# Constant matmuls in TensorE's early gaps, and an instruction order planned with them

## The chip, the core and the metric

The kernel runs on one core of a Trainium2 chip. The core has five engines that run side by side, each with its own instruction queue worked off in order: TensorE (PE in the profile; its weight loads are shown as PEld), VectorE (DVE), ScalarE (ACT), GpSimd (POOL) and SyncE (SP), which here only issues transfers between HBM and the on-chip memory SBUF. TensorE writes its results to another on-chip memory, PSUM, and VectorE or ScalarE copy them from there to SBUF.

The metric is the device time of one execution in microseconds (us). One execution is taken with a hardware profiler; its span goes from the first to the last instruction, and its own time is a little longer than its span.

## The reference

```python
x = A_q                                                    # (1, 2048, 640), bf16
k_shift = sum over t of k_pad[:, t:t+S, :] * shift_k[:, 3-t]     # a causal filter of 4 taps
kv = k_shift * v
y  = causal convolution of kv with ssm_k along the 2048 positions (by FFT of 4096, per channel)
h  = x + layernorm(x) * (y + kv * ssm_D)
h2 = h + (silu(layernorm(h) @ w_gate) * (layernorm(h) @ w_up)) @ w_down
```

There are 2048 positions of 640 channels. The feed-forward part has an inner width of 1728. Inputs and output are bf16.

## The kernel before

**Tiling.** The positions are cut into four blocks of 512 (block 0 to 3), each laid on 128 partitions as 4 slots of 640 channels. A block goes through a convolution stage (tags C0 to C3 in the code) and a feed-forward stage (F0 to F3).

**The convolution** is done in the frequency domain by matmuls with constant tables of cosines and sines. Each 512-position slice p of the filter ssm_k (tags G0 to G3) is loaded, folded by VectorE (`g_fold`, L701 to L713), turned by TensorE transposes into PSUM and copied out (`g_turn_pe`, L670 and L672), and transformed by matmuls with the table gb_t (`g_transform`, L736). For slice 0 the skip term ssm_D is added by one further matmul with the constant tile ones1, which has ones in its first row and zeros elsewhere. VectorE forms the 4 taps and the product with v (`shift`, L769 to L775). The product is transformed by matmuls with the table cs_t (`x_transform`: L792 for block 0, which also uses csm_t, the negated sines; L809 for the others). Copies out of PSUM go through one helper (`evac`, L437 on ScalarE, L443 on VectorE). VectorE multiplies spectra and adds them over earlier blocks; spectra that do not fit are written to HBM by GpSimd's queue and loaded again. `back` transforms back with the table ci_t (L901), scales and adds (L905, L909), takes the statistics of the layernorm (`ln_stats`: L838 and L840 on ScalarE, L849 to L852 on VectorE, the power -1/2 on GpSimd, L854), normalises (L921 or L924), and turns the result into the tile hlnT, by TensorE transposes for blocks 0 to 2 (L936), by transfers for block 3.

**The feed-forward stage** has 14 pieces of gate and up matmuls of 512 columns (L1009, ten for a full piece), ScalarE's silu and copy (L1013, L1014), VectorE's product (L1016), then the down matmuls (L1033, with h added through the identity in L1030 for blocks 0 to 2), ScalarE's copy out (L1038) and GpSimd's store.

**At the start** the four tap rows of shift_k, loaded into the first partition of a tile, are spread over the 128 partitions by eight matmuls with ones1 as weights (L529, 320 columns each) into four PSUM tiles, which are copied out as w, two by VectorE and two by ScalarE. ones1 is written by VectorE (L522, L523). ScalarE then takes the statistics of block 0's input (L838, L840 on wk), while VectorE forms the taps.

**Storage.** PSUM is used as four tiles of two banks (class `ps`). SBUF tiles belong to classes of a fixed count (five `wk`, three `wgu`, two `h`, and so on). Within every class except `ps`, tiles are handed out in the order in which the code creates them.

**The order of the work** is planned when the program is built. Every operation is put on record with its engine, a cost in us, what it reads and writes, and a priority; `DELTA` holds offsets to the priorities, one for a key of tag, engine and name, found beforehand. `Plan.schedule` is a list scheduler: for every engine it takes, among the operations whose inputs are done, the one that can start first, with lower priority number ahead on ties (with a slack of 0.05 us per unit of "slack SP", SP takes nearly always the lowest number). It keeps a clock per engine, starting at 0.6 us, and hands an operation a PSUM tile: of those free at its start, the one that came free last. TensorE's half-speed phase after a pause is modelled in four lines (`cold`). In the end the operations are sorted by planned start and issued in that order; each engine runs its own in that order on the chip, waiting by semaphores for what it needs.

Of the kernel before, what the change touches and what calls it, by code (L numbers as in the profile page):

```python
# [12 lines left out]
ACT = mybir.ActivationFunctionType  # L13
# [7 lines left out]
P = 128  # L21
# [6 lines left out]
GC = 256  # L28
NG = 7
DELTA = {  # L30
    "C0 ACT half": 5713,
    "C0 ACT lnh0": 1462,
    "C0 ACT y": 1339,
    "C0 ACT z": -2549,
    "C0 DVE eo0": -2261,
    "C0 DVE gate": -16818,
    "C0 DVE prod0": -14678,
    "C0 DVE tinyx": 31,
    "C0 PE inv0": -2297,
    "C0 SP ci_t": 16022,  # L40
    "C0 SP cs_t": 3931,
    "C0 SP gb_t": 1107,
    "C0 SP k": -728,
    "C0 SP v": -11,
    "C0 SP x": -2141,
    "C1 ACT hn": 2424,
    "C1 ACT xev1": -969,
    "C1 ACT y": -4984,
    "C1 DVE bfly0": -24238,
    "C1 DVE bfly1": -22972,  # L50
    "C1 DVE eo0": -3933,
    "C1 DVE eo1": -21519,
    "C1 DVE hmul0": -24066,
    "C1 DVE hmul1": -17335,
    "C1 DVE join0": -4523,
    "C1 DVE last": -3933,
    "C1 DVE nm": -14579,
    "C1 DVE prod": 733,
    "C1 DVE tinyh1": -3279,
    "C1 DVE xsum0": -3000,  # L60
    "C1 PE hTtr": -11983,
    "C2 ACT hn": -6262,
    "C2 DVE eo0": -12365,
    "C2 DVE eo1": -13863,
    "C2 DVE gate": -18349,
    "C2 DVE hmul0": -4317,
    "C2 DVE join0": -14364,
    "C2 DVE last": -99,
    "C2 DVE nm": 22411,
    "C2 DVE prod": -4774,  # L70
    "C2 DVE tinyx": -180,
    "C2 DVE xsum0": -668,
    "C2 DVE xsum1": -2435,
    "C3 ACT hn": -8326,
    "C3 ACT lnh0": 10,
    "C3 ACT lnh1": -9704,
    "C3 DVE bfly1": 20,
    "C3 DVE comb": 3729,
    "C3 DVE psum": -4522,
    "C3 DVE shift": 2173,  # L80
    "C3 DVE xsum1": 3949,
    "C3 PE x1": -26875,
    "C3 SP ldX": -5040,
    "F0 DVE ffn": -3823,
    "F0 PE down": 1944,
    "F0 SP w": 1894,
    "F1 PE down": 3501,
    "F2 DVE ffn": 2826,
    "G0 ACT gev": -234,
    "G0 DVE g_fold": -2452,  # L90
    "G0 DVE skip": -2446,
    "G0 PE g_transform": -10973,
    "G1 ACT gev": 13784,
    "G1 ACT half": 1293,
    "G1 DVE g_fold": -5018,
    "G2 ACT gev": 14649,
    "G2 DVE g_sum": 2060,
    "G2 PE g_turn_pe": 6402,
    "G3 DVE g_fold": -1695,
    "G3 DVE g_sum": 2144,  # L100
    "G3 PE g_transform": -6565,
    "slack SP": 3733,
}
OPT = (True, (0, 1, 2), (0,), (), (0, 1, 2), (1, 2, 3), True, (0,), (0,), 0, (0, 1, 2))

# [67 lines left out]


class Op:
    __slots__ = ("i", "eng", "dur", "fn", "deps", "succ", "allocs", "frees", "pri", "nwait", "ready", "soft", "alts", "key", "start", "end", "tag", "nbytes", "fix")


class Plan:
# [25 lines left out]
    def op(self, eng, dur, fn, r=(), w=(), pri=None, nbytes=0, alloc=(), alt=(), name=None, fix=None):  # L205
        o = Op()
        o.i, o.eng, o.dur, o.fn, o.nbytes = len(self.ops), eng, dur, fn, nbytes
        o.alts = [(eng, dur, fn)] + list(alt)
        o.fix = self.DMA_FIX if fix is None else fix
        o.pri = self.pri if pri is None else pri  # L210
        o.tag = self.tag
        o.key = f"{o.tag} {eng} {name or fn.__qualname__.split('.<locals>')[1 if fn.__qualname__.count('<locals>') > 1 else 0][1:]}"
        o.pri += DELTA.get(o.key, 0)
        o.deps, o.succ, o.soft, o.allocs, o.frees = set(), [], [], [], []
        for x, wr in [(x, False) for x in r] + [(x, True) for x in w] + [((b, 0), True) for b in alloc]:
            b, m = x if isinstance(x, tuple) else (x, -1)
            if b.cls is not None and o not in b.users:
                b.users.append(o)
            for i, bm, bw in b.log:
                if bm & m and (wr or bw):  # L220
                    o.deps.add(i)
            b.log.append((o.i, m, wr))
        o.deps.discard(o.i)
        self.ops.append(o)
        return o

    def schedule(self):
# [38 lines left out]
        while done < len(ops):  # L266
            best = None
            for e, lst in pend.items():
                cand = None
                t0 = clock[e]  # L270
                for o in lst:
                    st = max(t0, o.ready)
                    if o.nbytes:
                        st = max(st, flight[e != "POOL"][-8])
                        if e != "POOL":
                            st = max(st, hw_free)
                    ok = True
                    for b in o.allocs:
                        if not b.cls.startswith("ps") and fifo[b.cls][0] is not b and not (len(o.allocs) > 1 and b in fifo[b.cls][:len(o.allocs)]):
                            ok = False  # L280
                            break
                        if not free[b.cls]:
                            ok = False
                            break
                        st = max(st, min(free[b.cls])[0])
                    if not ok:
                        continue
                    key = (max(st, t0 + self.slack.get(e, 0)), o.pri, st, o.i)
                    if cand is None or key < cand[0]:
                        cand = (key, st, o, e)  # L290
                if cand and (best is None or cand[1] < best[1]):
                    best = cand
            if best is None:
                raise RuntimeError("plan stuck: " + repr([(e, [(o.i, o.tag, [b.name for b in o.allocs]) for o in l][:5]) for e, l in pend.items()])
                                   + repr({c: [b.name for b in f[:2]] for c, f in fifo.items()}))
            _, st, o, e = best
            o.eng, o.dur, o.fn = next(x for x in o.alts if x[0] == e)
            for b in o.allocs:
                if not b.cls.startswith("ps"):
                    fifo[b.cls].remove(b)  # L300
                k = min((x for x in free[b.cls] if x[0] <= st), key=lambda x: (-x[0], x[1]))
# [46 lines left out]
def kernel(  # L348
# [14 lines left out]
    nc = tc.nc  # L363
# [7 lines left out]
    psum = ctx.enter_context(tc.tile_pool(name="ps", bufs=1, space=bass.MemoryType.PSUM))  # L371
# [782 lines left out]
    order = pl.schedule()  # L1154
    with tc.manual_schedule():
        for o in order:
            o.fn()


# [28 lines left out]
```

## Time and profile before

| | |
|---|---|
| median of 8 runs | 297.24 us (295.34 to 297.82) |
| profiled execution: its own time | 296.66 us |
| profiled execution: span | 294.9 us |
| TensorE busy | 259.0 us, 1564 matmuls |
| VectorE busy | 217.5 us, 300 instructions |
| ScalarE busy | 213.4 us, 377 instructions |
| GpSimd busy | 31.2 us, 38 instructions |
| TensorE's first matmul | 3.10 us |
| TensorE's last matmul ends | 288.59 us |

A line of the summary gives an engine's busy time, its share of the span and its instructions. The row of digits under it cuts the span into 40 equal slices, and each digit is the busy share of a slice in tenths. A line of waits gives who waited for whom, the total in us, how many times, and the longest. The chain that ended last is followed back from the last instruction to whatever released it; its lines have a start, a length and what ran. In a timeline, "x16" merges 16 instructions, and a matmul's printed length includes its way through the array, so the pace of a row of matmuls is read from the distance of their starts. "L736" is a line of the kernel.

### The profile page before, as it was taken

The numbers are of one execution on the slowest core, as the hardware profiler recorded it, in microseconds if no ns is written. First come the engines' busy times: TensorE is split into PE (matmuls) and PEld (weight loads), VectorE is DVE, ScalarE is ACT, GpSimd is POOL, SyncE is SP. The second block draws the span as 40 slices with busy tenths as digits, with TensorE's granted clock in tenths as the row PEclk, the third lists the DMA queues.
The fourth block names the chain that finished last, engine by engine and source line by source line (L and its number), as shares of the span: only waits on it lengthen the run. The fifth ranks groups of instructions, "written<-read, shape, count | busy, mean of one in ns | idle before, by whom it ended". The sixth has DMA issues, their size and how long they took to land.

```text
span 294.9 us, 4255 instructions
## 1 busy us (share of the span) xinstructions
PE 259.0 (88%) x1564; PEld 150.2 (51%) x1564; DVE 217.5 (74%) x300; ACT 213.4 (72%) x377; POOL 31.2 (11%) x38
## 2 busy tenths in 40 slices
PE   3069998388999999899998998999999989999991
PEld 1046766154445576644444665654446754444670
DVE  5995999989999899899998998389998201121111
ACT  3588999989995978998558999961665973545321
POOL 2002001230102023011000030200000011000000
PEclk9999999869999999999999999999999999999998
DMA  7997158993994599934638798955563053550011
GB/s 228 344 372 243 50 226 258 373 380 129 293 329 103 185 353 390 381 103 133 153 71 240 233 314 314 327 195 134 114 177 89 2 133 106 145 129 0 2 44 46
DMA packets 59158, 57.83 MB, mean 196 GB/s; under 512 B 17729, under 2 KB 53762, under 8 KB 59138
## 3 DMA queue, kind: packets, MB, share of 16 engines
q1 hardware_dynamic: 57342, 47.08, 52.4%
q0 software_dynamic: 1792, 10.49, 9.5%
q8 instruction: 12, 0.20, 0.3%
q14 instruction: 8, 0.07, 0.1%
q10 hardware_dynamic: 4, 0.01, 0.0%
HBM read 45.76 MB, written 10.49 MB: 191 GB/s over the span
## 4 chain that ended last, share of the span: by engine, by line
ACT 36%; PE 30%; issue 19%; DVE 7%; DMA 5%; POOL 1%; SPq 1%; POOLq 0%; ACTq 0%; DVEq 0%
PE ps L1009 15%; ACT junk L838 6%; ACT lane L437 5%; PE ps L1033 5%; ACT junk L840 5%; PE ps L792 3%; DMA wk<-in_A_q_dram 3%; PE ps L736 3%; ACT s L905 3%; ACT sg L1013 2%; ACT s L921 2%; PE ps L809 2%; ACT uc L1014 2%; DMA lane<-xd 2%; ACT lane L745 2%
## 5 line engine op out<-in xcount | busy, mean ns | idle before, releaser
L1009 PE MATMUL ps<-hlnT,wgu 128*128 128x512 bf16 x540 | 119.0, 379 | 2.0 <-ACT uc L1014 1.1
L1009 PEld LDWEIGHTS <-wgu 128*128 128x128 bf16 x540 | 52.7, 98 | 66.1 <-issue 4.6
L1013 ACT ACTIVATE sg<-ps 128x512 bf16<-128x512 f32 (+1 forms) x56 | 33.6, 600 | 43.9 <-PE ps L1009 25.4
L1033 PE MATMUL ps<-wdA,tT 128*128 128x320 bf16 x384 | 55.6, 299 | 0.1
L1033 PEld LDWEIGHTS <-tT 128*128 128x128 bf16 x448 | 43.8, 98 | 17.4 <-issue 0.4
L1016 DVE TENSOR_TENSOR tT<-sg,uc 128x512 bf16<-128x512 bf16 (+1 forms) x56 | 22.8, 423 | 38.1 <-ACT uc L1014 37.9
L854 POOL TENSOR_TENSOR mv<-mv,mhalf 128x2 f32<-128x2 f32 (+1 forms) x12 | 18.6, 1552 | 146.7 <-DVE mv L850 81.4
L1014 ACT CAST uc<-ps 128x512 bf16<-128x512 f32 (+1 forms) x56 | 32.7, 584 | 0.3 <-PE ps L1009 0.2
L437 ACT CAST lane<-ps 128x640 bf16<-128x640 f32 x42 | 27.2, 745 | 0.9 <-PE ps L792 0.9
L1122 DVE TENSOR_TENSOR lane<-lane,lane 128x3840 bf16<-128x3840 bf16 x12 | 25.8, 2154 | 0.5 <-DMA lane<-hd 0.3
L736 PE MATMUL ps<-wgu,gb_t 128*128 128x320 bf16 x128 | 22.3, 312 | 3.8 <-ACT wgu L672 2.7
L769 DVE TENSOR_TENSOR wk<-krun,w 128x2560 bf16<-128x2560 bf16 (+1 forms) x20 | 24.0, 1220 | 0.0
L1038 ACT ACTIVATE o<-ps,mean 128x640 bf16<-128x640 f32 x16 | 12.5, 787 | 14.4 <-PE ps L1033 14.4
L809 PE MATMUL ps<-wk,cs_t 128*128 128x320 bf16 x96 | 17.1, 326 | 6.6 <-DVE wk L775 4.9
L901 PE MATMUL ps<-eo,ci_t 128*128 128x320 bf16 x128 | 18.7, 299 | 1.6 <-DMA wgu<-in_B_w_up_dram 1.0
L736 PEld LDWEIGHTS <-gb_t 128*128 128x128 bf16 x128 | 12.9, 101 | 11.2 <-issue 4.4
L774 DVE TENSOR_TENSOR wk<-wk,wk 128x2560 bf16<-128x2560 bf16 (+1 forms) x15 | 18.0, 1220 | 0.0
L901 PEld LDWEIGHTS <-ci_t 128*128 128x128 bf16 x128 | 12.5, 98 | 7.0 <-issue 1.9
L809 PEld LDWEIGHTS <-cs_t 128*128 128x128 bf16 x96 | 9.8, 104 | 12.1 <-DVE wk L775 5.2
L838 ACT ACTIVATE junk<-wk 128x640 bf16<-128x640 bf16 x16 | 11.9, 747 | 4.7 <-DMA wk<-in_A_q_dram 4.5
L905 ACT ACTIVATE s<-ps,one,mv 128x640 bf16<-128x640 f32 x15 | 13.3, 921 | 1.8 <-POOL mv L854 0.9
L838 ACT ACTIVATE junk<-h 128x640 bf16<-128x640 bf16 x16 | 12.0, 749 | 2.0 <-DVE h L909 1.5
(94 smaller groups left out, 311.4 us busy)
## 6 DMA issues: line engine op xcount, KB each, us to landing
wgu<-in_B_w_gate_dram SPq DMA_DIRECT2D x24, 320.0 KB, 3.3
wgu<-in_B_w_up_dram SPq DMA_DIRECT2D x24, 320.0 KB, 4.5
lane<-xd SPq DMA_DIRECT2D x6, 960.0 KB, 5.6
lane<-hd SPq DMA_DIRECT2D x6, 960.0 KB, 7.8
xd<-lane POOLq DMA_DIRECT2D x4, 960.0 KB, 5.1
hd<-lane POOLq DMA_DIRECT2D x4, 960.0 KB, 7.1
krun<-in_A_k_dram SPq DMA_DIRECT2D x4, 640.0 KB, 6.8
wk<-in_A_v_dram SPq DMA_DIRECT2D x4, 640.0 KB, 8.8
```

The costliest lines, as they stand in the source:

```text
L437: nc.scalar.copy(dst(), src())
L736: nc.tensor.matmul(ps.t[:, h, 0:NH], wt, mv, start=(k == 0), stop=(k == len(ks) - 1))
L769: nc.vector.tensor_mul(dst.t[:, sl, :], ks, w4.t[:, j:j + 1, :].broadcast_to([P, n, D]))
L809: nc.tensor.matmul(ps.t[:, h, 0:NH], cs_t.t[:, s, n, c * P:(c + 1) * P], kv.t[:, s, h * NH:(h + 1) * NH], start=(a == 0), stop=(a == 1))
L838: act(0.73, lambda s=s: nc.scalar.activation(junk.t[:], x.t[:, s, :], ACT.Identity, scale=-1.0 / D, accum_out=mv.t[:, s:s + 1]), [(x, 1 << ...
L901: nc.tensor.matmul(ps.t[:, hh, 0:NH], ci_t.t[:, c, 1 - n, s, :], x.t[:, 2 * pos[n] + c, hh * NH:(hh + 1) * NH], start=(k == 0), stop=(k == 3))
L1009: nc.tensor.matmul(q(ps.t[:, k, 0:w]), wg.t[:, kt, off:off + P], rr(hT.t[:, kt, :]), start=(kt == 0), stop=(kt == NDC - 1))
L1013: act(c_act(w) + 0.02, lambda ps=ps, sg=sg, np_=np_, w=w: nc.scalar.activation(sg.t[0:np_, 0:w], ps.t[0:np_, 0, 0:w], ACT.Silu), [(ps, 1)] ...
L1014: act(c_act(w), lambda ps=ps, uc=uc, np_=np_, lo=up_lo, k=len(offs) - 1, w=w: nc.scalar.copy(uc.t[0:np_, 0:w], ps.t[lo:lo + np_, k, 0:w]), ...
L1016: dve(c_tt(w), lambda sg=sg, uc=uc, c=c, np_=np_, w=w, rr=rr, q=q: nc.vector.tensor_mul(rr(tv()[0:np_, c, :]), q(sg.t[0:np_, 0:w]), q(uc.t ...
L1033: nc.tensor.matmul(ps.t[:, hh, 0:NH], tv()[:, c, m * P:(m + 1) * P], wdc(c)[:, hh * NH:(hh + 1) * NH], start=(c == 0 and not oadd), stop=( ...
L1122: dve(c_tt(6 * D), lambda xl=xl, hl=hl: nc.vector.tensor_mul(xl.t[:], xl.t[:], hl.t[:]), [xl(), hl()], [xl()], name="prod")
```

## The change

Three things are changed. Before an operation of TensorE that the plan starts more than 0.8 us after TensorE's last one, and that takes a new PSUM tile, a number of matmuls are issued into the first half of that same tile: weights ones1, and ones1 repeated four times as the 512 columns. What they write is overwritten by the operation itself. Their number is worked out in the plan from the planned start, the moment the tile came free, and 0.22 us for one. The model of the half-speed phase is changed: it now counts only a pause that can't be filled so, of over 2.5 us, and lasts 4.5 us instead of 2.6. And the table of offsets is another one.

```diff
-    "C0 SP ci_t": 16022,
-    "C0 SP cs_t": 3931,
-    "C0 SP gb_t": 1107,
...
+    "C0 DVE eo0": -46193,
+    "C0 SP cs_t": 6082,
+    "C0 SP k": -10520,
+    "C0 SP v": -3881,
+    "C0 SP x": -5367,
+    "C2 SP ldX": -18099,
+    "C3 DVE prod": -117764,
+    "G0 ACT turn": -130,
+    "G0 DVE g_fold": -302,
+    "slack SP": 13090,
...
-        o.deps, o.succ, o.soft, o.allocs, o.frees = set(), [], [], [], []
+        o.deps, o.succ, o.soft, o.allocs, o.frees, o.warm = set(), [], [], [], [], 0
...
                 b.slotno = k[1]
+                b.since = k[0]
             o.start = st
             if e == "PE":
-                if st - clock[e] > 2.0:
-                    cold = st + 2.6
+
+                since = max([b.since for b in o.allocs if b.cls == "ps"] or [st])
+                lo = max(min(since, st), clock[e])
+                if lo - clock[e] > 2.5:
+                    cold = st + 4.5
+                o.warm = max(0, int((st - 0.4 - lo) / 0.22)) if st - clock[e] > 0.8 else 0
                 if st < cold:
                     o.dur = 2 * o.dur if st + 2 * o.dur <= cold else o.dur + (cold - st) / 2
...
         for o in order:
+            if o.warm:
+                ps = next(b for b in o.allocs if b.cls == "ps")
+                for _ in range(o.warm):
+                    nc.tensor.matmul(ps.t[:, 0, :], ones1.t[:], ones1.t[:].unsqueeze(1).broadcast_to([P, 4, P]), start=True, stop=True)
             o.fn()
```

Of the table's 72 old entries no value is kept; there are now 71, and 39 of the keys are in both tables. Among those that change the early loads, gb_t had 1107 and ci_t 16022 and have none now; cs_t had 3931 and has 6082; x had -2141, v -11 and k -728.

More of the change, by code (lines that the diff above doesn't have):

```diff
@@ L30 @@
 DELTA = {
[L31 to L39, printed above, removed]
-    "C0 SP ci_t": 16022,
-    "C0 SP cs_t": 3931,
-    "C0 SP gb_t": 1107,
[L43 to L102, printed above, removed]
+    "C0 ACT half": 2346,
+    "C0 ACT lnh0": -4201,
+    "C0 ACT lnh1": 267,
+    "C0 ACT z": 2693,
+    "C0 DVE comb": -6557,
+    "C0 DVE eo0": -46193,
@@ new lines @@
+    "C0 DVE eo1": -42546,
+    "C0 DVE g_sum": -11140,
+    "C0 DVE hmul1": -5850,
+    "C0 DVE prod0": -7150,
+    "C0 DVE tinyh1": -4004,
+    "C0 DVE xsum0": -6521,
+    "C0 DVE xsum1": -7151,
+    "C0 SP cs_t": 6082,
+    "C0 SP k": -10520,
+    "C0 SP v": -3881,
+    "C0 SP x": -5367,
+    "C1 ACT lnh0": -703,
+    "C1 DVE bfly0": 2804,
+    "C1 DVE bfly1": 3910,
+    "C1 DVE hmul0": -2731,
+    "C1 DVE join0": 2763,
+    "C1 DVE nm": 1961,
+    "C1 DVE shift": -5091,
+    "C1 PE inv0": -645,
@@ new lines @@
+    "C1 PE x0": -6101,
+    "C1 PE x1": -5811,
+    "C2 ACT lnh0": 1469,
+    "C2 ACT xev1": -7949,
+    "C2 DVE comb": -3190,
+    "C2 DVE hmul0": 5660,
+    "C2 DVE join0": -5850,
+    "C2 DVE last": -5005,
+    "C2 DVE psum": -3425,
+    "C2 DVE shift": 13818,
+    "C2 DVE xsum1": 2712,
+    "C2 PE inv0": -4890,
+    "C2 PE inv1": -18283,
+    "C2 SP ldX": -18099,
+    "C3 ACT hn": -2883,
+    "C3 ACT lnh1": -11795,
+    "C3 ACT y": -31,
+    "C3 ACT z": 3587,
+    "C3 DVE bfly1": 10377,
+    "C3 DVE prod": -117764,
@@ new lines @@
+    "C3 DVE psum": -997,
+    "C3 DVE shift": 6430,
+    "C3 PE x0": -4100,
+    "C3 PE x1": -11395,
+    "F0 ACT down": 6357,
+    "F0 DVE ffn": 1595,
+    "F0 PE down": 8281,
+    "F1 PE down": -2369,
+    "F1 PE up": -5390,
+    "F1 SP w": -10659,
+    "F2 DVE ffn": 7428,
+    "G0 ACT gev": -10019,
+    "G0 ACT turn": -130,
+    "G0 DVE g_fold": -302,
+    "G0 DVE skip": -10032,
+    "G0 PE g_transform": -3886,
+    "G1 ACT half": 584,
+    "G1 DVE g_sum": -12973,
+    "G2 ACT gev": 5469,
+    "G2 DVE g_fold": -10045,
@@ L103 @@
+    "G2 DVE g_sum": -1071,
+    "G2 PE g_turn_pe": 13004,
+    "G3 DVE g_sum": -43,
+    "G3 PE g_transform": -23314,
+    "slack ACT": 4,
+    "slack SP": 13090,
 }
@@ L175 @@
 class Op:
-    __slots__ = ("i", "eng", "dur", "fn", "deps", "succ", "allocs", "frees", "pri", "nwait", "ready", "soft", "alts", "key", "start", "end", "tag", "nbytes", "fix")
+    __slots__ = ("i", "eng", "dur", "fn", "deps", "succ", "allocs", "frees", "pri", "nwait", "ready", "soft", "alts", "key", "start", "end", "tag", "nbytes", "fix", "warm")
 class Plan:
```

## The prediction

> **What bounds the kernel now.** I read the engine summary first, then the list of waits of TensorE, the chain that ended last, the timeline of TensorE, and a table of stages. The summary says who is full.
>
> ```profile
> span 294.9 us, 4255 instructions
> PE 259.0 (88%) x1564; PEld 150.2 (51%) x1564; DVE 217.5 (74%) x300; ACT 213.4 (72%) x377; POOL 31.2 (11%) x38
> PE   3069998388999999899998998999999989999991
> ```
>
> TensorE is busy 259.0 of 294.9 us, so about 36 us are without it: 3.1 before its first matmul, 8.7 and 2.3 up to 18.76 us, some 6.5 between there and 58.52 (one wait of 4.9), and 6.3 at the end (its last matmul ends at 288.59, then copy, add, store). Some 9 us are left for the 230 us between, in waits of about 1 us at most. From 60 us on TensorE is nearly full; what remains to be had is ahead of that. The waits name the gaps:
>
> ```profile
> PE ps L670 <- ACT junk L840: 8.7, 1, 8.7
> PE ps L809 <- DVE wk L775: 4.9, 1, 4.9
> PE ps L529 <- DMA hlnT<-in_A_shift_k_dram: 3.1, 1, 3.1
> PE ps L736 <- ACT wgu L672: 2.7, 2, 2.3
> ```
>
> The columns are the total, the number of times and the longest. The first is put down to ScalarE, but the weight load of the same transposes waited 9.3 us for VectorE's fold (L702), which is the real releaser. The chain tells what the gaps delay:
>
> ```profile
> 2.66 8.04 DMA wk<-in_A_q_dram
> ...
> 17.60 1.12 ACT wgu L672
> 18.76 5.45 PE ps L736 x24
> 24.21 1.09 PE ps L792 x8
> 25.29 2.17 PE ps L736 x16
> 27.47 6.55 PE ps L792 x48
> ...
> 60.62 3.36 PE ps L809 x12
> ```
>
> From 18.76 to 35 us the chain is TensorE alone. But 24 matmuls of 320 columns take 5.45 us at 18.76 and 16 of the same size take 2.17 us at 25.29. That is 0.267 us apart (three in 0.80 us) against 0.136: after a gap the array runs at half rate for about 4 us, here until about 22.7. The granted clock reads 1.00 before 57 us, though the matmuls at 18.76 are slow, so there I go by spacing. At the second gap it does show it; the columns are the stretch, its length, PE, PEld, DVE, ACT and POOL busy with their instructions, the clock, DMA share and GB/s:
>
> ```profile
> 56.00:57.00 1.00, 0.00 (x0) 0.00 (x0) 0.90 (x4) 0.97 (x3) 0.00 (x0) 1.00 1.02 410
> 57.00:58.00 1.00, 0.00 (x0) 0.00 (x0) 1.00 (x2) 0.97 (x3) 0.85 (x1) 0.53 0.99 399
> 62.00:63.00 1.00, 1.00 (x6) 0.52 (x5) 0.75 (x3) 0.62 (x2) 0.21 (x1) 0.50 1.17 317
> 63.00:64.00 1.00, 1.00 (x7) 0.64 (x6) 1.00 (x4) 0.64 (x1) 0.00 (x0) 0.56 1.22 335
> ```
>
> TensorE stopped at 53.65 us. The clock fell to half at about 57.1, 3.4 us later, and came back at about 63.9, 5.4 us after work resumed at 58.52 (with a hole of 0.85 us in it).
>
> **The change, part by part.** (1) Number of fills. It is int((start - 0.4 - lo) / 0.22), where lo is the later of TensorE's last end and the moment the PSUM tile came free. The planner's times are not in the trace; I put the measured ones in. First gap: lo is 0.6 (the planner's first clock), start 3.10, so 9 fills. Second: the last copy of w leaves PSUM at 6.25 (5.56 + 0.69), start 14.18, so 34. Third, 16.49 to 18.76: the scheduler takes the tile that came free last, which is the one that the copy L672 has just emptied, so 0; that idle of 2.27 us is under the 3.4 after which the clock fell. Fourth, 53.65 to 58.52: 20. Together 63 fills, 126 instructions with their weight loads, if the order stays alike.
>
> (2) Price of a fill. None is in the trace. Warm, the nearest row is L1009, the same 128x512: 60 matmuls from 79.80 to 92.75 are 0.216 each, what the 0.22 assumes. Half clock: 0.267 x 512/320 = 0.43 each, an estimate from the spacing at 18.76. The weight load (98 ns) lies beside the matmul.
>
> (3) First gap, a cost. The constant tile is written by VectorE until 2.13 us, and the 9 fills run at half clock: 2.2 + 9 x 0.43 = 6.1. The eight matmuls of L529, now at 3.10, queue behind them, 3.0 late. If the clock has opened after about 4 us of fills they take 8 x 0.136 = 1.1 instead of 2.4. VectorE's two copies of w (0.82 each) then end near 8.3 rather than 5.81, so the first tap multiply of the convolution (5.73) starts about 2.5 later. Bounds: 0 (if the planner puts the first start earlier) and 3.0.
>
> (4) Who pays for that. VectorE is full from 5.7 to 22.8, then idles 3.14 us until 25.94, waiting for TensorE. The gated product ends at 19.54 and TensorE first reads it at 24.04: 4.5 us of cover. With 2.5 late, the product is there at 22.0. The fold comes 2.5 late too, 16.6 instead of 14.1; the transposes (20 in 2.31 us, 0.11 apart, warm 0.065 by the ten at 35.11 in 0.72 us) half done at 17.3; the copy L672 1.17; so the L736 matmuls start near 18.6, as now. The 34 fills, from about 8.7 on, end at 8.7 + 34 x 0.217 = 16.1, inside this. I cost it at 0; if the cover is gone it costs up to 2.5.
>
> (5) Warm start of L736, the main gain: 24 x 0.136 = 3.3 instead of 5.45, so 2.1 off the chain; the transform of x starts near 22 rather than 24.04. Bounds 0 (ScalarE must carry the copies: it idles only 2 us in all between 20 and 35) and 2.15. I take 2.1, because the chain there is TensorE's alone.
>
> (6) Fourth gap: 16 matmuls of L809, 4 at 58.52 and 12 at 60.62 (3.36 us). Warm the twelve take 1.8, so 1.6 less. But the path into the gate and up matmuls runs through VectorE's normalisation (L924), which waits for GpSimd's power until 62.22 whatever TensorE does; the transposes L936 come at 63.5 and could come near 62.6. I take 1.0, bounds 0 and 1.6.
>
> (7) The order. Read from the table of offsets: loads of gb_t and ci_t go ahead of the second ssm_k slice, cs_t last; v stays ahead of x although x's offset is lower, because their class of tiles is handed out in order of creation. cs_t gets 0.5 MB more ahead of it, about 1.5 us at the 330 to 400 GB/s of this stretch: it landed at 18.7 (10.72 + 8.0), then at about 20.2, still before 22. The copy L672 gets an offset that puts it ahead of ScalarE's statistics of x (until 17.6), up to 1.9 off the start of L736 if the fold is not late; part (4) makes it late, so 0. What the other 60 or so offsets do can't be read off. Bound from the trace: a wait as long as the longest repairable one (4.9) goes, or one of that size comes. I take 0.
>
> Sum on the profiled execution (296.66, span 294.9): 0 - 2.1 - 1.0 + 0 = -3.1, so 293.6. The median of the eight is 297.24, 0.6 above it: 294.1, rounded to **294.0**.
>
> The Trainium skill ("TensorE: Matmul & The Clock Gate", "What's actually happening") holds that the array runs at half clock until about 3.4 us of sustained work, in a window that runs free of the kernel, and that idle of one such window throttles it again. The fall 3.4 us after 53.65 agrees; the return after 5.4 us is longer. This speaks for keeping TensorE busy and against the planner's flat 0.22 for a fill that is itself cold. The same section puts the ramp's penalty below 1% of a typical span, which by that rule would cap what warming saves at 2.9 us, 293.8 for the profiled run; the rows alone gave 293.6. The same page ("Part 4: PE-mode transpose") says transposes do not get the full clock; the ten at 35.11, 0.072 apart against 0.11 at 14.18, contradict it, and by that rule part (4) would be some 0.4 longer.
>
> **Rivals.**
> A. *The gain ends in another wait; no change.* The last feed-forward block starts at 243.83 after a wait of 0.79 us for its transposed input, and the 45 us behind that are TensorE alone. That input comes down a chain of VectorE and ScalarE from 217.9 on. If that chain does not move, because VectorE (90.8 of the 95 us from 65 to 160 busy) starts 2.5 late and only gets its 3.14 back, TensorE merely waits 3.9 at this point instead of 0.8. For it: VectorE's net gain is 0.6. Against it: VectorE idles 5.6 us between 180 and 200, so it is not the bound there. Time: 297.24 - 0.6 = 296.6.
> B. *Slower, at the same place.* The new order brings the last block's input later. TensorE has no other work left at 243.8, so every microsecond that this input comes behind 243.8 is one at the end. It decides once the delay exceeds the 3.1 gained upstream, in that TensorE waits there longer than 3.9. By the bound of part (7), 4.9 late: 297.24 + 4.9 = 302.1; half of it, the middle between none and the bound, gives 299.7. For it: the offsets of blocks 2 and 3 are nearly all new. Against it: nothing in the trace.
> C. *The order gains on its own.* The L809 wait at 53.65 goes and the head delay does not occur: 294.0 - 4.9 + 1.0 (no longer to be had) - 1.9 = 288.2.
> D. *The fills do not open the clock*, so the change does not do what it says. Then 34 x 0.43 = 14.6 us from 8.7 on end at 23.3; the transposes, copy and L736 come behind that, 26 instead of 18.76: +7, so 304.
>
> **Numbers.** What a measurement can tell from no change is 0.5%, 1.5 us: faster is below 295.75, slower above 298.73. Forecast (292 to 295.7) 0.36, A 0.16, B 0.30, C 0.14, D 0.04. Faster is 0.36 + 0.14 = 0.50; same 0.16; slower 0.34. The range goes from C's 288 to B's 302, which leaves out D, the far ends of B and C. The forecast's own range is 292 to 295.7.
>
> **What would show it.** Right: some 60 fills before 60 us; fills 0.43 apart first, then 0.217; L529 near 6 us and VectorE's first tap near 8; L736's first 24 matmuls in about 3.3 us; no half clock near 58 us; the first matmul of the x transform near 22 us; the last feed-forward's start some 3 us before 243.8. Wrong: if L529 starts at 3.1, part (3) failed; if L736 is warm but starts later than 19, part (4); if the x transform is 2 us early and the last block's first matmul is not, A or B; if fills stand among matmuls after 65 us, my count is off, and each costs 0.217 on the fullest engine.

## The result, and the profile after

The change makes the kernel slower: 299.12 us median (22 runs, 297.47 to 299.49) against 296.82 for the kernel before beside it (62 runs); ratio of the times 1.0071, interval 1.0057 to 1.0084. The forecast of 294.0 was wrong. The rows below answer to those shown of before; the diff adds lines, so that L529 is now L533, L670 is L674, L672 is L676, L736 is L740, L809 is L813 and L1009 is L1013, and the fills are L1164. First the summary.

```profile
span 297.4 us, 4334 instructions
PE 272.3 (92%) x1614; PEld 155.9 (52%) x1614; DVE 215.6 (73%) x297; ACT 215.3 (72%) x380; POOL 29.1 (10%) x38
PE   7989996599998999899999989699999978999991
```

The span is 2.5 us longer. TensorE has 50 matmuls more, the fills, and is busier by 13.3 us although it does no more of the work: its busy share says less than it did. Then its waits, and its timeline (start, length, what ran, times, and the idle time ahead of it):

```profile
PE ps L740 <- ACT wgu L676: 5.6, 3, 4.5
PE ps L1013 <- ACT hlnT L948: 3.8, 2, 2.8
...
PE ps L1013 <- DMA hlnT<-s: 1.6, 1, 1.6
```

```profile
2.18 3.59 PE L1164 MATMUL ps<-ones 128*128 128x512 bf16 x9 [2.18 <-DVE ones L527]
5.70 2.42 PE L533 MATMUL ps<-hlnT,ones 1*128 1x320 bf16 x8
8.47 9.83 PE L1164 MATMUL ps<-ones 128*128 128x512 bf16 x37 [0.35 <-DVE w L447]
18.14 1.28 PE L674 MATMUL ps<-ident,wk 128*128 128x128 bf16 x20
20.18 0.43 PE L740 MATMUL ps<-wgu,gb_t 128*128 128x320 bf16 x2 [0.76 <-ACT wgu L676]
...
53.90 4.43 PE L740 MATMUL ps<-wgu,gb_t 128*128 128x320 bf16 x16 [4.46 <-ACT wgu L676]
59.58 1.86 PE L1164 MATMUL ps<-ones 128*128 128x512 bf16 x4 [1.25 <-ACT lane L441]
...
189.19 7.24 PE L1013 MATMUL ps<-hlnT,wgu 128*128 128x512 bf16 x25 [2.80 <-ACT hlnT L948]
...
246.39 29.30 PE L1013 MATMUL ps<-hlnT,wgu 128*128 128x512 bf16 x135 [1.63 <-DMA hlnT<-s]
```

The long early waits are gone from the list, since the fills stand where they were. But the matmuls of the tap rows start at 5.70 instead of 3.10, the transposes at 18.14 instead of 14.18, and the slice-0 transform at 20.18 instead of 18.76. It runs warm there (24 matmuls from 20.18 to 23.43). Two new waits have come, 4.46 us ahead of 53.90 and 2.80 ahead of 189.19, and the last feed-forward block starts at 246.39 instead of 243.83. The granted clock (the column after POOL's) behind the second new wait:

```profile
189.00:190.00 1.00, 0.81 (x3) 0.34 (x3) 0.10 (x2) 1.00 (x4) 0.00 (x0) 0.76 1.02 146
190.00:191.00 1.00, 1.00 (x4) 0.32 (x3) 0.14 (x2) 1.00 (x2) 0.79 (x1) 0.50 0.59 192
```

An idle time of 2.80 us was followed by half clock: 25 matmuls of 512 columns took 7.24 us; the same 25 took 5.79 in e1 below, where the clock did not fall there.

ScalarE's list of waits has a row that was not there before, with the total, the times and the longest as above:

```profile
ACT wgu L676 <- PE ps L674: 2.9, 1, 2.9
```

ScalarE now waits for the slice-0 transposes; before, their results lay in PSUM until ScalarE was done with its statistics (the last transpose ended at 16.49, the copies began at 17.50).

### The profile page after: what moved, and what is told of

Read it like the earlier page. It is cut to its first block, busy times and chain, and to the rows that moved or that the text cites. A ratio compares the mean times of both kernels' runs of the same rounds, so it can differ in the third digit from the quotient of the medians.

```text
span 297.4 us, 4334 instructions
## 1 busy us (share of the span) xinstructions
PE 272.3 (92%) x1614; PEld 155.9 (52%) x1614; DVE 215.6 (73%) x297; ACT 215.3 (72%) x380; POOL 29.1 (10%) x38
## 4 chain that ended last, share of the span: by engine, by line
PE 42%; ACT 36%; issue 19%; DVE 1%; POOL 1%; POOLq 0%; ACTq 0%
PE ps L1013 24%; ACT lane L441 7%; ACT junk L842 5%; PE ps L1164 5%; ACT junk L844 5%; PE ps L1037 4%; PE ps L813 3%; ACT s L909 3%; ACT s L925 2%; ACT wgu L676 2%; PE ps L905 2%; ACT o L1042 2%; ACT h L891 2%; ACT sg L1017 2%; ACT uc L1018 2%
## 5 line engine op out<-in xcount | busy, mean ns | idle before, releaser
L1013 PE MATMUL ps<-hlnT,wgu 128*128 128x512 bf16 x540 | 120.1, 383 | 6.6 <-ACT hlnT L948 3.8
L1013 PEld LDWEIGHTS <-wgu 128*128 128x128 bf16 x540 | 53.2, 99 | 71.5 <-issue 8.8
L858 POOL TENSOR_TENSOR mv<-mv,mhalf 128x2 f32<-128x2 f32 (+1 forms) x12 | 16.5, 1378 | 132.9 <-DVE mv L854 98.8
L1126 DVE TENSOR_TENSOR lane<-lane,lane 128x3840 bf16<-128x3840 bf16 x12 | 25.8, 2156 | 2.7 <-DMA lane<-hd 1.6
L740 PE MATMUL ps<-wgu,gb_t 128*128 128x320 bf16 x128 | 22.3, 320 | 5.7 <-ACT wgu L676 5.6
L1042 ACT ACTIVATE o<-ps,mean 128x640 bf16<-128x640 f32 x16 | 12.4, 786 | 13.4 <-PE ps L1037 13.3
L740 PEld LDWEIGHTS <-gb_t 128*128 128x128 bf16 x128 | 13.2, 103 | 13.2 <-issue 6.5
L1164 PE MATMUL ps<-ones 128*128 128x512 bf16 x50 | 15.3, 475 | 3.8 <-DVE ones L527 2.2
L905 PE MATMUL ps<-eo,ci_t 128*128 128x320 bf16 x128 | 18.6, 299 | 0.1
L778 DVE TENSOR_TENSOR wk<-wk,wk 128x2560 bf16<-128x2560 bf16 (+1 forms) x15 | 18.1, 1221 | 0.0
L813 PE MATMUL ps<-wk,cs_t 128*128 128x320 bf16 x96 | 14.3, 298 | 1.0 <-ACT o L1042 0.9
L1130 DVE TENSOR_TENSOR lane<-lane,lane 128x3840 bf16<-128x3840 bf16 x6 | 12.9, 2153 | 0.0
```

The lines of the kernel that those rows point to most:

```text
L740: nc.tensor.matmul(ps.t[:, h, 0:NH], wt, mv, start=(k == 0), stop=(k == len(ks) - 1))
L905: nc.tensor.matmul(ps.t[:, hh, 0:NH], ci_t.t[:, c, 1 - n, s, :], x.t[:, 2 * pos[n] + c, hh * NH:(hh + 1) * NH], start=(k == 0), stop=(k == 3))
L1013: nc.tensor.matmul(q(ps.t[:, k, 0:w]), wg.t[:, kt, off:off + P], rr(hT.t[:, kt, :]), start=(kt == 0), stop=(kt == NDC - 1))
L1126: dve(c_tt(6 * D), lambda xl=xl, hl=hl: nc.vector.tensor_mul(xl.t[:], xl.t[:], hl.t[:]), [xl(), hl()], [xl()], name="prod")
L1164: nc.tensor.matmul(ps.t[:, 0, :], ones1.t[:], ones1.t[:].unsqueeze(1).broadcast_to([P, 4, P]), start=True, stop=True)
```

## The experiments

Twelve runs, each beside the kernel before on its own chip. The table holds the ratio to it, and the starts (us, from each run's profile) of the tap rows' matmuls, the slice-0 transposes, the slice-0 transform, the x transform of block 0, and the feed-forward stages F0, F2 and F3. The starts are those of one execution each. In the profiles of the changed kernel, e4, e8 and e9 the clock fell at F2, in that of e7 just behind it, in the others not; in the new order that alone moves F3 by some 1.6 us.

| run | ratio (interval) | taps | transp. | slice 0 | x | F0 | F2 | F3 |
|---|---|---|---|---|---|---|---|---|
| before | 1 | 3.10 | 14.18 | 18.76 | 24.04 | 67.61 | 189.06 | 243.83 |
| changed | 1.0071 (1.0057 to 1.0084) | 5.70 | 18.14 | 20.18 | 25.62 | 67.93 | 189.19 | 246.39 |
| e1, new order, no fills | 1.0034 (1.0005 to 1.0063) | 2.35 | 14.41 | 16.97 | 23.69 | 66.77 | 187.95 | 243.37 |
| e2, old order, fills | 0.9996 (0.9972 to 1.0019) | 6.01 | 18.23 | 20.27 | 23.52 | 66.42 | 187.58 | 243.42 |
| e3, old order, no head fills, 25 | 0.9965 (0.9943 to 0.9986) | 3.10 | 14.18 | 18.91 | 24.89 | 67.42 | 188.59 | 243.39 |
| e4, new order, no head fills, 25 | 0.9982 (0.9956 to 1.0009) | 2.36 | 14.37 | 16.75 | 22.79 | 64.41 | 185.59 | 242.62 |
| e5, as e3, third gap filled | 0.9927 (0.9907 to 0.9946) | 2.99 | 14.36 | 18.99 | 22.24 | 64.79 | 185.98 | 241.33 |
| e6, old order, head fills only | 1.0004 (0.9986 to 1.0022) | 6.14 | 17.22 | 19.78 | 24.86 | 68.34 | 189.96 | 244.74 |
| e7, new order, copies earlier | 0.9991 (0.9962 to 1.0019) | 3.09 | 15.43 | 17.46 | 22.90 | 65.98 | 185.40 | 244.49 |
| e8, new order, no head fills, 37 | 0.9966 (0.9948 to 0.9983) | 3.04 | 15.54 | 17.58 | 23.02 | 65.31 | 186.49 | 243.54 |
| e9, changed again | 1.0068 (1.0042 to 1.0093) | 5.95 | 18.39 | 20.43 | 25.87 | 67.80 | 189.01 | 246.22 |
| e10, as e8, gap of F2 filled | 0.9929 (0.9909 to 0.9950) | 3.10 | 15.63 | 17.67 | 23.11 | 65.42 | 186.62 | 242.12 |
| e11, new order, 4 head fills | 1.0012 (0.9992 to 1.0032) | 4.00 | 17.16 | 19.19 | 24.63 | 66.27 | 187.47 | 242.91 |
| e12, as e10, gap of L676 filled | 0.9960 (0.9934 to 0.9985) | 3.01 | 15.92 | 17.95 | 23.40 | 65.35 | 186.56 | 242.03 |

Two theories stood at the outset. **M**: the new order loses the time at its two long waits, and the fills net about nothing. **R**: the fills lose it, because 9 of them hold back the head of the kernel by 2.6 us.

### e1: the new order without fills

```diff
-            if o.warm:
+            if False:
```

> The changed order with no fill issued. Theory M (the order's waits after 45 us lose the time: 4.5 us for the copy L676 at 49.4 and 2.8 for hlnT at 186.4, each with a half-clock stretch behind it; the fills' early gain is eaten by their own 2.6 us at the head and 1.6 at the transposes, so they net about nothing): 298.5 to 300, within 0.7 of the changed kernel; tap multiplies start at 5.7 again, the L740 matmuls near 17.2 but at half rate, the x transform near 24.8; both long waits are still there. Rival R (the fills are what costs, because VectorE starting 2.6 us late reaches the end; the order is harmless): 296.5 to 297, like the kernel before.

296.82 us, ratio 1.0034: between the two theories. The order does cost, some 1.0 us (0.1 to 1.9 by the interval), about half of the whole; the rest is the fills. In the profiled execution (296.15 us, one of its shorter ones) the start is better than before: slice 0 at 16.97, because the copy L676 stands ahead of the last two of ScalarE's eight statistics passes, and F0 0.8 earlier. Both long waits are there, and F2 to F3 takes 55.4 us instead of 54.8.

### e2: the old order with fills by the same rule

```diff
+                since = max([b.since for b in o.allocs if b.cls == "ps"] or [st])
+                lo = max(min(since, st), clock[e])
+                o.warm = max(0, int((st - 0.4 - lo) / 0.22)) if st - clock[e] > 0.8 else 0
```

(The issuing of the fills is as in the change; the model of the half-speed phase and the offsets are those of the kernel before, and with them the order. The edits of e3, e5 and e6 come on top of this one.)

> The old order, unchanged, with fills put in by the same rule (9, 34 and 22 of them). Theory M: the head delay of 2.6 us is absorbed by VectorE's idle time at 22.8 us, L736 starts near 19.7 instead of 18.8 but warm, the stretch after 58 us runs warm: 1 to 2 us faster than before, ratio 0.993 to 0.997. Rival R: the late VectorE reaches the end, 1.5 to 2.6 us slower than before, ratio 1.005 to 1.009.

296.05 us, ratio 0.9996: no gain and no loss; R's 1.5 to 2.6 us are excluded, M's 1 to 2 us as well, if barely. The starts are what M said: slice 0 at 20.27 but warm, x at 23.52, and from the C1 x transform (58.34) to F0 8.1 us instead of 9.1, since the 22 fills kept that stretch warm. F2 is 1.5 us early, but F3 only 0.4 (243.42): TensorE waits 1.88 us there for the last block's input, 0.79 before. That is the place of rival A.

### e3: the old order, no fills at the head, 25 ahead of the transposes

```diff
+            o.warm = {9: 0, 34: 25}.get(o.warm, o.warm)
             if o.warm:
```

> As the old order with fills, but none ahead of L533's counterpart at the head, and 25 instead of 34 ahead of the transposes, which allows for the first nine or so running at half rate. Theory M: first tap at 5.7, transposes near 14.2, L736 at 18.8 and warm, warm at 58 us: the 3.1 us of the prediction, ratio 0.988 to 0.992. Rival R, in which only the head delay costs: also faster, but by no more than 1 us. A third outcome, that nothing early reaches the end because the last feed-forward block still waits for its input near 244 us: ratio 1.000.

295.18 us, ratio 0.9965, a third of what the forecast had promised for this. The profile tells where the rest went. The fills ended in time and the transposes ran warm (their second ten start at 15.20 and take 0.73), and then TensorE idled 2.98 us until 18.91, where the slice-0 transform ran at half rate after all. Clock in the column after POOL's:

```profile
15.00:18.00 3.00, 0.73 (x10) 0.66 (x11) 3.00 (x6) 2.90 (x9) 0.00 (x0) 0.95 1.11 372
18.00:19.00 1.00, 0.09 (x1) 0.09 (x1) 1.00 (x3) 1.00 (x2) 0.00 (x0) 0.50 0.98 361
24.00:25.00 1.00, 1.00 (x7) 0.65 (x6) 0.00 (x0) 0.60 (x1) 0.00 (x0) 0.75 0.99 365
```

A mean of 0.95 over the first three us puts the fall at 17.7, 1.8 us after the last transpose (15.93); it came back at 24.5.

### e4: the new order, no fills at the head, 25 ahead of the transposes

```diff
+            o.warm = {9: 0, 37: 25}.get(o.warm, o.warm)
             if o.warm:
```

> The changed kernel without its 9 fills at the head and with 25 instead of 37 ahead of the transposes; its 4 late ones kept. Theory M: L740 near 17.2 and warm, the x transform near 22.7 instead of 25.6, but the copy L676 and the waits at 49 and 186 us stay; one or two of the three microseconds arrive: 297 to 298.5. Rival R: below the kernel before, 295 to 296.5.

295.83 us, ratio 0.9982, within R's range: taking fills away gains 0.9% on the changed kernel. In this order 25 are too few: they end at 12.0, TensorE idles 2.39 us until 14.37, and the transposes are at half rate again.

### e5: as e3, the third gap filled too

```diff
+            if o is g0[0]:
+                ps = g0[1].allocs[-1]
+                for _ in range(12):
+                    nc.tensor.matmul(ps.t[:, 0, :], ones1.t[:], ones1.t[:].unsqueeze(1).broadcast_to([P, 4, P]), start=True, stop=True)
```

(g0 are the slice-0 transforms in the planned order; the fills go into the tile of the second one, which is free, while that of the first has just been emptied.)

> The old order with the 25 and 22 fills of the earlier run without a head, and 12 more (12 x 0.217 = 2.6 us) between the transposes and L736, written into the PSUM tile of the second L736 group, which is free. Theory M, now with a second clause (an idle of 2.4 to 3 us can already cost the clock, so the unfilled third gap is where the early gain was lost): L736 starts near 18.8 and warm, its 24 matmuls take 3.3 us, x transform near 22.2 instead of 24.9; about 2 us below the run without these 12, ratio to before 0.988 to 0.992, and a narrower spread. Rival S (what is gained early is taken back by the wait of the last block's input near 244 us): the start is earlier as said, but the ratio stays at 0.995 to 0.998.

294.44 us, ratio 0.9927 (0.9907 to 0.9946), 2.2 us below before. From the timeline:

```profile
15.95 2.75 PE L1165 MATMUL ps<-ones 128*128 128x512 bf16 x12
18.99 0.43 PE L740 MATMUL ps<-wgu,gb_t 128*128 128x320 bf16 x2 [0.28 <-ACT wgu L676]
...
22.24 1.25 PE L796 MATMUL ps<-wk,cs_t 128*128 128x320 bf16 x8
```

The slice-0 transform starts no earlier than before (18.99), but its 24 matmuls take 3.25 us instead of 5.45 and x starts at 22.24. Slice 0 gives x 1.8 us, the fourth gap F0 another 1.0: F0 is 2.8 earlier than before, F3 2.5 (241.33), the time 2.2 (1.6 to 2.8). Nearly all of it arrives, and S falls. These are the warm parts of the prediction, on the order for which they were worked out, without its fills at the head and with the third gap filled.

### e6: the old order with the head fills alone

```diff
+            o.warm = {9: 9}.get(o.warm, 0)
             if o.warm:
```

> The old order with only the 9 fills at the head. First tap multiply at 8.3 instead of 5.7. Theory M: VectorE's idle time from 22.8 to 25.9 takes most of it; 0 to 0.7 us slower than before, ratio 1.000 to 1.0025. Rival R: VectorE late to the end, 1.5 to 2.6 us slower, ratio 1.005 to 1.009.

296.56 us, ratio 1.0004. The tap rows are 3.0 late and so are the transposes (17.22), but the slice-0 transform is only 1.0 late (19.78), because in the old order the copy L676 waits behind all eight statistics passes of ScalarE anyway; F3 is 0.9 late in this profile, the longest of its twelve executions (297.57). With slice 0 at half rate as before, the old order hides most of the head fills.

### e7: two copies earlier in ScalarE's queue

```diff
     order = pl.schedule()
+    turn = [o for o in order if o.key == "G2 ACT turn"][-1]
+    turn.start = 45.85
+    tr, hT = [o for o in order if o.key == "C2 PE hTtr"][0], [o for o in order if o.key == "C2 ACT hT"][0]
+    tr.start, hT.start = 174.37, 174.38
+    order.sort(key=lambda o: (o.start, o.i))
```

(And 0 fills at the head, 32 ahead of the transposes.)

> The changed order, no fills at the head, 32 ahead of the transposes, and two copies put earlier in ScalarE's queue: the copy L676 of slice 2 ahead of three statistics, and block 2's first copy L948 (with its transposes) ahead of two statistics and a copy out. Theory M (the order loses its time at these two waits, because statistics cost ScalarE more than they were planned at): the wait of 4.5 us at 51 shrinks below 2, that of 2.8 us at 186 below 1 and no half clock follows; 2 to 4 us below the changed order without head fills, ratio to before 0.984 to 0.992. If the waits shrink and the time does not, the last block's input sets the end: ratio 0.996 to 1.000.

296.79 us, ratio 0.9991. Both waits shrank, the first from 4.46 to 2.02, the second from 2.78 to 1.01 with no half clock behind it, and F2 starts at 185.40. The time did not follow:

```profile
185.40 4.48 PE L1013 MATMUL ps<-hlnT,wgu 128*128 128x512 bf16 x19 [1.01 <-DVE hlnT L949]
191.95 2.08 PE L1013 MATMUL ps<-hlnT,wgu 128*128 128x512 bf16 x5 [2.08 <-ACT uc L1018]
```

A new wait of 2.08 us stands ahead of 191.95, for copies of ScalarE that now come after the statistics which were put off; the clock falls at 192.2 (0.60 over 192 to 193, then 0.50), and F3 comes at 244.49. M's claim that moving these two copies brings 2 to 4 us is wrong: ScalarE is nearly full in both places (6.91 of the 7 us from 45 to 52, 13.67 of the 14 from 178 to 192), and what is taken from one wait is paid at another.

### e8: the changed kernel without its 9 head fills, and nothing else

```diff
+            o.warm = {9: 0}.get(o.warm, o.warm)
             if o.warm:
```

> The changed kernel without its 9 fills at the head, everything else kept, the 37 fills too. They start 2.6 us earlier, at 5.1, nine of them at half rate (3.9), 28 at 0.217 (6.1), so they end near 15.1, 0.7 behind the fold. If the head is what costs (2.6 us behind for VectorE in an order that has no room for it): 296 to 297, like the run without head and with 25. If the count of 37 costs as much as the head: 297.5 to 298.5.

295.02 us, ratio 0.9966. Leaving out nine matmuls of 0.43 us turns a loss of 0.7% into a gain of 0.3%, more than either expectation.

```profile
3.04 2.42 PE L533 MATMUL ps<-hlnT,ones 1*128 1x320 bf16 x8 [3.04 <-DMA hlnT<-in_A_shift_k_dram]
5.81 9.90 PE L1165 MATMUL ps<-ones 128*128 128x512 bf16 x37 [0.35 <-DVE w L447]
15.54 1.28 PE L674 MATMUL ps<-ident,wk 128*128 128x128 bf16 x20
17.58 0.43 PE L740 MATMUL ps<-wgu,gb_t 128*128 128x320 bf16 x2 [0.76 <-ACT wgu L676]
```

Every start in the table is 2.6 to 2.9 us ahead of the changed kernel's, from the tap rows (3.04 against 5.70) to F3 (243.54 against 246.39): the delay at the head goes through 240 us undiminished. Both profiles have the half clock at F2, so that is not what sets them apart. The count of 37 does no harm beside 25 (e4), within the intervals.

### e9 and e11: the changed kernel again, and with 4 head fills

```diff
+            o.warm = {9: 4}.get(o.warm, o.warm)
             if o.warm:
```

> The changed kernel as it is, beside the three below on one chip. Theory H, formed from the eight runs so far: the 9 fills at the head cost the changed order 2.6 to 3 us from start to end, because nothing in it waits for anything else in the first 60 us (VectorE 24.0, ScalarE 24.9 of 25 us busy from 20 to 45), while the old order hid them behind ScalarE's statistics. Ratio 1.005 to 1.009 again.

> The changed kernel with 4 fills at the head instead of 9: they end at 2.2 + 4 x 0.427 = 3.9, some 0.8 behind the arrival of the tap rows. Theory H (every microsecond at the head is one at the end): 0.8 us above the kernel without head fills (ratio 0.9966) and 2.2 below the changed kernel, ratio 0.999 to 1.000. Rival (the head costs by a threshold, in that a late start makes a transfer or a clock window be missed): like one of the two, 0.9966 or 1.007.

298.75 us, ratio 1.0068, for the changed kernel once more; 297.25 us, ratio 1.0012, with four (0.9992 to 1.0032). With 0, 4 and 9 head fills the ratio goes 0.9966, 1.0012, 1.0068: it rises with each step, and the interval at four overlaps neither end's, so it is not one threshold. H's 0.999 to 1.000 for four lies at the low end of the interval. In the profiles the tap rows are 0.96 later with four than with none, and F0 0.96. (F3 is 0.6 earlier, because the clock fell at F2 in the profile with none and not in this one.)

### e10 and e12: the gaps of the new order filled too

```diff
+            for _ in range({779: 11}.get(o.i, 0)):
+                nc.tensor.matmul(pl.cls["ps"][0][0][:, 0, :], ones1.t[:], ones1.t[:].unsqueeze(1).broadcast_to([P, 4, P]), start=True, stop=True)
```

(Operation 779 is block 2's first gate and up matmuls; e12 has 157: 19 as well, the slice-2 transform behind the copy L676. PSUM tile 0 is free at both. No head fills in either.)

> The changed kernel without head fills, and with 11 more (2.4 us) in the idle time of 2.8 us ahead of block 2's gate and up matmuls, in a PSUM tile that is free. If that idle time costs the clock in most executions and 1.6 to 1.8 us at the end: the two groups of times of the kernel without head fills (294.4 to 295.3 at a mean clock of 0.99, 296.0 to 296.7 at 0.973) become one, mean clock above 0.985, ratio 0.990 to 0.994. If the last block's input sets the end: 0.996 to 0.998.

> As the one before, and 19 fills (4.1 us) in the wait of 4.5 us for the copy L676 near 47 to 51. The stretch from 51 to 60, at half clock without them, runs warm. If TensorE's pace there matters: another 1 to 1.5 us, ratio 0.985 to 0.990. If ScalarE (4.9 of 5 us busy there) sets it: 0 to 0.5 us, ratio as without them.

e10: 294.41 us, ratio 0.9929 (0.9909 to 0.9950). The stretch behind F2, first without and then with the 11 fills:

```profile
188.00:190.00 2.00, 2.00 (x6) 0.68 (x5) 1.56 (x1) 1.31 (x2) 0.54 (x1) 0.50 0.90 374
```

```profile
188.00:190.00 2.00, 2.00 (x11) 0.90 (x10) 1.54 (x1) 2.00 (x5) 0.68 (x1) 1.00 0.87 347
```

Six matmuls at half clock have become eleven at full clock, F2 to F3 takes 55.5 us instead of 57.1, and the single executions, which without these fills lie at 294.4 to 295.3 (mean clock 0.99) or 296.0 to 296.7 (0.973), now lie at 294.2 to 295.1. The mean clock did not rise with them as expected: four of the six have 0.975 or 0.976. In the profile (0.976) the half clock stands from 50.5 to 60.7 alone, the stretch that e12 warms, so the mean clock of an execution does not tell its time.

e12: 294.92 us, ratio 0.9960, no better; two of its twelve executions took 297.5, which no profile shows. The slice-2 transform does run warm:

```profile
47.06 4.26 PE L1163 MATMUL ps<-ones 128*128 128x512 bf16 x19
51.68 2.33 PE L740 MATMUL ps<-wgu,gb_t 128*128 128x320 bf16 x16 [0.36 <-ACT wgu L676]
57.36 1.30 PE L1167 MATMUL ps<-ones 128*128 128x512 bf16 x4 [3.34 <-ACT lane L441]
```

But TensorE then waits 3.34 us for ScalarE's copies of its results instead of 1.25, and F0 comes at 65.35 as against 65.42. ScalarE, busy for 12.9 of the 13 us from 45 to 58, sets that stretch; TensorE's pace there is worth nothing.

## Why the prediction was wrong, step by step

The sum of the runs: the new order alone +0.34%, its fills without the head ones -0.68% (e8 against e1), the head fills +1.05% (changed against e8). In us of the kernel before that is +1.0, -2.0 and +3.1, where the prediction had 0, -3.1 and 0. The term that was mis-sized most is the head fills, part (4).

1. *The number of fills.* Foreseen 9, 34, 0 and 20, found 9, 37, 0 and 4: the rule was read rightly for an order alike, and in the old order the numbers are 9, 34, 0 and 22 (e2). In the new order the longest late gap lies elsewhere, ahead of the slice-2 transform; by the rule it gets none where its PSUM tile has only just been emptied.
2. *Price of a fill.* 0.427 at half clock and 0.217 at full, as estimated.
3. *The head.* The tap rows were foreseen near 6, found at 5.70, the first tap multiply near 8.2, found at 8.34. Part (3) had the eight tap matmuls at half clock, to be faster once it opens. They are not bound by it: the clock opened at 5.20 (fills start at 4.71 and 5.14, 0.43 apart, then at 5.39, 0.25 later), and yet they start 0.28 apart and take 2.42, as before. The nine fills bought nothing for the 37 either: the clock fell again at 8.61, and some eight of the 37 ran at half rate in the changed kernel, about as many as in e8, which has no head fills.
4. *"I cost it at 0", the step that failed.* The nine head fills cost 3.1 us by the ratios, 2.85 at F3 in the profiles (246.39 against 243.54 of e8), beyond even the bound of 2.5. The cover was taken from the profile of before: VectorE's 3.14 us at 22.8, and a slice-0 transform that nothing could bring ahead of 18.76. The new order had spent that cover: the copy L676 no longer stands behind all statistics, and slice 0 could start at 16.97 (e1). Part (7) saw this move and put it at 0, since part (4) made the fold late; so one slack was written down twice, as the cover of the delay and as an earlier start that is merely not had. The sign that the prediction itself gave for part (4), L736 warm but later than 19, came true (20.18). The busy times from 20 to 45 us, of before, of the changed kernel and of e2, in this order, show what is left to give:

```profile
20.00:45.00 25.00, 24.34 (x182) 16.79 (x181) 21.69 (x36) 22.64 (x32) 2.80 (x3) 1.00 0.54 195
20.00:45.00 25.00, 24.30 (x188) 17.06 (x188) 24.00 (x39) 24.89 (x39) 2.46 (x3) 1.00 0.61 212
20.00:45.00 25.00, 23.87 (x189) 16.78 (x189) 24.76 (x40) 23.82 (x34) 2.80 (x3) 1.00 0.59 211
```

VectorE is busy for 21.69 us before and for 24.00 in the changed kernel, ScalarE for 22.64 and 24.89. Nor does the cover hold in the old order once slice 0 runs warm: in e2 VectorE is busy for 24.76, because it comes later and part (5) takes away the very wait for TensorE that part (4) counted as cover. With the head fills alone, slice 0 still cold, the old order hides most (e6, 1.0004). With all fills by the rule it gains nothing (e2, 0.9996, slice 0 at 20.27 where part (4) had 18.6); with none at the head, 25 instead of 34 ahead of the transposes and the third gap filled, 0.69% more (e5, slice 0 at 18.99, F3 2.1 earlier). What the head alone is of that 0.69% was not measured.
5. *The fills ahead of the transposes* were foreseen to end at 16.1, inside the cover. They ended at 18.1, 1.6 behind the fold (16.55): some eight of them ran at half clock, which part (4) had not counted, as the clock fell at 8.61 and came back at 12.02. Without head fills the same 37 still hold the transposes back (15.54 in e8 against 14.41 in e1), and yet are worth it, since slice 0 then runs warm and x starts at 23.02 instead of 23.69.
6. *The warm start of slice 0* was right in size: 24 matmuls in 3.25 us (3.3 foreseen), 2.2 less than before; in e5 1.8 of it are left at x and nearly all of that arrives. But part (1) let the third gap pass with "under the 3.4 after which the clock fell". That was one fall in one trace, and the gap grew from 2.27 to 2.98 us as the transposes ahead of it got faster. In e3 the clock fell 1.8 us into it, and the gain was lost there; filling it (e5) took the ratio from 0.9965 to 0.9927.
7. *The fourth gap*, 1.0 foreseen: in the old order the stretch shrank from 9.1 to 8.1 us (e2, e3). In the new order that stretch is set by ScalarE and the gain is nil (e12).
8. *The order*, taken at 0 with bounds of 4.9 either way, costs 1.0 us (e1). Part of that price may be the 2.8 us wait ahead of F2, which can cost the clock: with fills, F2 to F3 took 1.6 us less in e10's profile than in e8's. The ratios give e10 0.37% over e8, but their intervals just touch and e12, with the same fills at F2, shows no gain over e8; the groups of e8's times (four of twelve executions 1.5 us longer) would account for some 0.5 us, an estimate. In e1's own profile the clock did not fall at F2, and what sets its longer executions (298.3 to 299.1, beside 296.1) was not caught in a profile and is open.

Rival B, the last block late, named the place (246.39 against 243.83) and nearly the price, 299.7, but by luck: its condition, a wait of more than 3.9 us there, did not come (1.63), and its cause is not the one: with the same order and no head fills F3 comes at 243.54. The input was late because everything was, from 3 us on.

The two fastest versions are the old order with fills in the second, third and fourth gaps (e5, 0.9927), and the new order without head fills and with the gap of F2 filled (e10, 0.9929, though e12, which has these fills too, stands at 0.9960). e3 and e8 also lie below the kernel before, by 0.3%.

## What to carry to other kernels

A filler on an in-order engine is free only as long as it ends before the work behind it is ready; count it by the rate at which it will itself run, and put none ahead of the first operation that everything else follows from. When a change brings a new order, slack that was measured in the old order is no cover: name which engine owns it in the new one, and do not book the same slack twice: a wait that one part of the change removes is no cover for another part. Filling a gap is worth something where the engine's pace sets the stretch behind it, and nothing where another engine does, however cold the clock.

## What the runs showed of the hardware

The time from the last matmul to the fall of the granted clock was no constant: about 1.8 us (e3, at 17.7), 2.3 (e7, at 192.2), 2.6 (e4, at 14.6), 3.1 (changed, at 189.5) and 3.4 (before, at 57.1). Neither was the return: 3.0 us after the first fill in the changed kernel (5.20), 3.7 behind 189.19, 5.6 behind 18.91 in e3. The changes themselves have a pattern: in each of the fourteen profiles they lie whole multiples of 3.41 us apart (5.20, 8.61 and 12.02 in the changed kernel; 22.93, 57.06 and 63.89 before), on a grid that lies elsewhere in each execution. What decides is how much TensorE worked in the 3.41 us that end at such a point. Four of these stretches, of e7, e1, e3 and e4 (the first number behind the length is TensorE's busy time):

```profile
188.78:192.19 3.41, 1.33 (x8) 0.51 (x6) 2.36 (x2) 3.41 (x7) 0.67 (x1) 1.00 0.97 347
183.48:186.89 3.41, 1.69 (x25) 1.49 (x23) 2.04 (x3) 3.32 (x9) 0.52 (x1) 1.00 0.90 284
17.68:21.09 3.41, 2.18 (x9) 1.25 (x9) 3.38 (x6) 2.69 (x4) 0.00 (x0) 0.50 1.06 376
14.61:18.02 3.41, 3.30 (x24) 2.34 (x22) 3.38 (x7) 3.25 (x6) 0.00 (x0) 0.50 1.11 339
```

At the end of the first (39% busy) the clock fell, of the second (50%) it stayed; at the end of the third (64%) it stayed at half, of the fourth (97%) it opened. Over all fourteen profiles every fall came behind a busy share of 0.41 or less and none behind 0.45 or more, and every opening behind 0.78 or more, the tap matmuls left out. The transposes count in this (they are over half of the fourth stretch), the tap matmuls, which read one partition, do not: from 5.20 to 8.61 in the changed kernel TensorE was busy for 3.06 us, 2.42 of them with these, and the clock fell. So whether a gap of 2 to 3 us costs the clock depends on where it lies on the grid, and differs from one execution to the next: the gap of 2.8 us ahead of F2 cost it in the profiles of the changed kernel, e4, e8 and e9, and did not in those of e1 and e11. Up to the first recorded change the profile reads 1.00 although the matmuls run at half rate, so the first opening is read from their spacing.

The times of the changed kernel fall into groups by mean clock: of its 22 executions ten with 0.984 or more took 297.5 to 298.6 us, twelve with 0.975 or less 299.1 to 299.5. For e10 and the kernel before the mean clock tells no such thing (beside e1 the latter took 295.0 to 298.0 at 0.984 to 0.986).

The Trainium skill ("TensorE: Matmul & The Clock Gate", "What's actually happening") holds that the gate watches a window that runs free of the kernel, which agrees with this grid and this spread. Its advice to avoid idle gaps of more than about 3 us (the same page, "Why this matters for your kernels") is too lenient by these runs: 2.1 us (e7), 2.4 us (e4) and 2.8 us (changed) cost the clock here.
